# Moving the build of a table of picked positions on VectorE from behind normalised rows to between two steps of the second batch's scores

## The chip, the cores and the metric

The kernel runs on one core of one Trainium2 chip. The metric is the time of one execution on the device in microseconds (us); lower is better. Before the change three runs took 340.24, 340.25 and 340.36 us (median 340.25).

## The reference

Sparse attention with a window and a few global positions is followed by a two-layer network with softplus between the layers. Cut to what matters:

```
B, H, S, D = 8, 8, 576, 64;  8 global positions (global_idx);  window = 32
scores = (q @ k.T) / sqrt(D)
mask = (|i - j| <= window) | is_global[i] | is_global[j]
attn = softmax(where(mask, scores, -1e9))
x = (attn @ v), heads side by side: 4608 tokens x 512
out = softplus(x @ w_in) @ w_out          # 512 -> 2048 -> 512
```

## The kernel before

**Tiles and stages.** The 4608 tokens are cut into 9 phases of 512 tokens. A phase is four steps (n) of four blocks of 32 rows, each with all eight heads. One step of the attention goes through all engines in turn:

- TensorE computes the scores of the step into PSUM (s, L1106).
- VectorE adds the mask and writes the sum to SBUF (st, L1110, two per step), then takes row maxima (m, L1123).
- GpSimd subtracts the maxima (st, L1129).
- ScalarE takes exponentials (st, L1146).
- VectorE sums and inverts (sm, L1153; rs, L1155).
- GpSimd multiplies by the inverse: these are the normalised rows (pn, L1161). There are two buffers of them.
- VectorE transposes them (pt, L1170).
- TensorE multiplies the transposed rows with the values (xo, L1280), once for several steps together. VectorE and ScalarE cast the result (xT, L733).

The rows of the global positions have scores of their own (sg, L999; pg, pgt, ov, odd, vg). Behind xo, the network runs on TensorE (h, L1315, then o, L1326), with softplus on ScalarE (g, L1321). The steps of the attention of the next phase lie between the matmuls of the network of this one.

**Loading.** SyncE's queue loads q and k of batches 2 to 7 and v of batches 2 to 7 as 32-bit numbers (stage). GpSimd and ScalarE cast them to 16 bits (qb, kb, vb; L733, L730, L726), VectorE transposes q and k (qx, L851; kx, L855). GpSimd's queue brings the weights, the first two batches' v (vb, L477) and most of the output (L1338).

**The table of picked positions.** From batch 2 on, the keys and queries of the eight global positions are picked out of kb and qb by a matmul with a table of zeros and ones (pick, L904). `make_pick` (L597 to L606) builds this table once for all batches, with eight instructions on VectorE: a memset of the table (L545, by the helper `clear`), three small operations (L599 to L601), and four comparisons (L604), one for each quarter of the partitions, of positions (posK) with the global indices (gf), both in SBUF:

```
for r in range(R):
    V.tensor_tensor(out=pick[quad(r)]...[:, :, r * NG:(r + 1) * NG],
                    in0=posK[quad(r)]..., in1=gf[quad(r)]..., op=OP.is_equal)
```

Its first reader is the picking of batch 2 (`pck`, L898).

**What sets the order.** The kernel registers some 1700 pieces of work with their dependences, and a table of numbers, `ORDER`, says in which order they are taken: a number is five times the piece, plus the engine (0 TensorE, 1 ScalarE, 2 VectorE, 3 GpSimd, 4 DMA). `make_pick` is piece 37, registered at L1421, so that its number is 187: piece 37 on VectorE. `_Order.run` (L202) walks through the table, gives each piece a planned time from costs (1800 ns for `make_pick`) and a PSUM bank, and emits the pieces in the order of planned times. Every engine executes its instructions strictly in that order; semaphores hold an instruction until its inputs are there.

Of the kernel before, what the change touches and what calls it, by code (L numbers as in the profile page):

```python
# [307 lines left out]
def kernel(  # L308
# [61 lines left out]
        690, 1111, 1116, 986, 1031, 1040, 648, 653, 658, 663, 668, 783, 193, 542, 562, 1021, 1071, 1026, 1076, 1045, 700, 710, 720, 730,  # L370
        1036, 677, 697, 687, 717, 567, 1056, 1051, 706, 771, 1080, 1085, 740, 737, 1720, 727, 1091, 1732, 1096, 750, 760, 776, 1160, 1727,
        766, 746, 1140, 1165, 855, 757, 1145, 871, 1151, 1171, 1156, 866, 1176, 862, 877, 1765, 1810, 1180, 1360, 1320, 1822, 1737, 1772, 1777,
        1817, 1782, 1240, 1365, 1370, 1375, 1325, 1185, 1200, 1205, 1245, 1210, 1215, 1330, 1335, 1196, 1236, 1191, 1250, 1900, 1912, 1855, 1867, 1351,
        1226, 1255, 1346, 1356, 1341, 1120, 1125, 1280, 1285, 1450, 1290, 1295, 1231, 1266, 1271, 1276, 1131, 1261, 1301, 1221, 1311, 1136, 1316, 1907,
        1862, 788, 1965, 1455, 1460, 1465, 1380, 1630, 1385, 1635, 1470, 793, 798, 1948, 1953, 1306, 1640, 1540, 1390, 1645, 1475, 1480, 1650, 1655,
        1545, 1395, 1400, 1660, 1550, 1485, 1743, 1958, 1963, 1788, 1490, 1495, 1405, 1410, 1415, 1500, 1917, 1827, 1833, 1972, 1872, 1878, 1746, 1976,
        1982, 1665, 1985, 1505, 1420, 1791, 1425, 1510, 1670, 1675, 1430, 1435, 1680, 1515, 1752, 1797, 1758, 1803, 1991, 1881, 1997, 2001, 1762, 2005,
        2017, 1836, 1923, 2021, 2744, 2026, 2011, 1520, 1525, 1555, 1560, 1565, 1570, 1887, 1842, 1532, 1807, 1442, 2140, 2060, 1685, 2145, 2065, 2070,
        2150, 2180, 1848, 1893, 2185, 1575, 1580, 2155, 2075, 2190, 1585, 2100, 2105, 2110, 2195, 1926, 2086, 2081, 2161, 2096, 187, 1590, 1595, 2176,
        2115, 2136, 2126, 2171, 2166, 2131, 1600, 1605, 1610, 1690, 1695, 1700, 1448, 2758, 1705, 2380, 2385, 1615, 2201, 2206, 2091, 2121, 1852, 1897,  # L380
        2030, 2035, 1932, 2749, 2390, 2395, 2400, 1712, 2047, 2057, 2753, 2041, 2051, 2405, 2410, 2415, 2270, 2310, 2420, 2763, 1938, 1718, 2766, 2994,
        2216, 2211, 2777, 2772, 2780, 2786, 2276, 2260, 2790, 2266, 2796, 2370, 2230, 2802, 1942, 2316, 2376, 1621, 2236, 2805, 2850, 2220, 2250, 2340,
# [1123 lines left out]
```

## Time and profile before

| | |
|---|---|
| median of three runs | 340.25 us (340.24 to 340.36) |
| profiled execution | 341.66 us, of which the span is 339.9 us |
| TensorE matmul busy | 323.5 us, 95% of the span |
| VectorE busy | 230.6 us, 68% |
| ScalarE busy | 218.5 us, 64% |
| GpSimd busy | 204.7 us, 60% |
| granted TensorE clock, mean | 0.990 |

The span runs from the first to the last instruction of the profiled execution; the rest of its time lies around it. PE is TensorE's matmuls, PEld its weight loads, DVE is VectorE, ACT ScalarE, POOL GpSimd, SP SyncE, and a q behind the name is the engine's queue. A row of a timeline has the start in us from the span's start, the duration in us, engine, line, operation, output<-inputs, shape, the number of instructions merged in it, and in brackets the idle time of the engine ahead of it with what ended it. A row of waits has the engine and line that waited, what released it, the total in us, how often, and the longest. A wait that no semaphore in the profile explains is put down to "issue". The shares in the chain say what the path that ended last consisted of. Spans on GpSimd are rough, and busy time on TensorE is not work at its peak, since matmuls are pipelined.

### The profile page before, as it was taken

How to read it: one execution, taken by the hardware profiler on the slowest of the kernel's cores; microseconds unless marked ns; L12 is line 12 of the kernel's file. 1: busy time of each engine (PE TensorE's matmuls, PEld its weight loads, DVE VectorE, ACT ScalarE, POOL GpSimd, SP SyncE). 2: the span in 40 equal slices, each digit the busy share in tenths (PEclk: the TensorE clock that was granted, in tenths of full speed). 3: DMA queues.
4: the chain of work that ended last, by engine and by line, in shares of the span. 5: the costliest groups of instructions: out<-in, count | busy, mean ns of one | idle time of the engine just before them, and what ended most of it. 6: DMA issues, size and time to landing. Idle time of an engine off the chain costs nothing.

```text
span 339.9 us, 12052 instructions
## 1 busy us (share of the span) xinstructions
PE 323.5 (95%) x5277; PEld 173.5 (51%) x5277; DVE 230.6 (68%) x400; ACT 218.5 (64%) x438; POOL 204.7 (60%) x185
## 2 busy tenths in 40 slices
PE   8889979967999999899999999999999999999996
PEld 3547866543545545454445445444544454454543
DVE  6886768898796899974888558597689563342000
ACT  4789628542596969377866674898258656934531
POOL 6899746795189449679578679587058609060000
PEclk9999999995999999999999999999999999999999
DMA  6999999999903979989989991341001002000102
GB/s 181 167 187 170 169 165 142 153 185 184 183 10 62 170 153 209 151 166 194 206 158 175 204 202 52 73 128 38 4 33 62 3 35 93 33 31 33 64 33 91
DMA packets 172391, 40.36 MB, mean 119 GB/s; under 512 B 161460, under 2 KB 168884, under 8 KB 172340
## 3 DMA queue, kind: packets, MB, share of 16 engines
q1 hardware_dynamic: 145908, 23.61, 40.7%
q0 software_dynamic: 24560, 12.85, 25.4%
q10 hardware_dynamic: 1872, 3.15, 2.4%
q8 instruction: 41, 0.67, 0.9%
q14 instruction: 10, 0.08, 0.1%
HBM read 36.71 MB, written 9.44 MB: 136 GB/s over the span
## 4 chain that ended last, share of the span: by engine, by line
PE 86%; DVE 7%; DMA 2%; SPq 2%; ACT 2%; issue 1%
PE o L1326 36%; PE h L1315 36%; PE xo L1280 5%; PE s L1106 3%; DVE pick L604 2%; DMA stage<-in_q_dram 2%; PE ov L1028 2%; ACT st L1142 1%; PE pick L904 1%; DVE pt L1170 1%; SPq L530 1%; PE sg L999 1%; SPq L523 1%; DVE m L1121 1%; DVE sm L1153 1%
## 5 line engine op out<-in xcount | busy, mean ns | idle before, releaser
L1326 PE MATMUL o<-wout,g 128*128 128x512 bf16 (+1 forms) x592 | 138.5, 376 | 1.2 <-issue 1.2
L1321 ACT ACTIVATE g<-h 128x512 bf16<-128x512 f32 (+3 forms) x192 | 83.9, 496 | 47.1 <-PE h L1315 44.2
L1161 POOL TENSOR_TENSOR pn<-st,rs 128x1024 bf16<-128x1024 f32 (+1 forms) x36 | 64.8, 1810 | 42.4 <-DVE rs L1155 40.0
L1326 PEld LDWEIGHTS <-g 128*128 128x128 bf16 x592 | 56.0, 98 | 63.5 <-issue 3.4
L1129 POOL TENSOR_TENSOR st<-st,m 128x1024 f32<-128x1024 f32 x32 | 60.6, 1898 | 40.7 <-DVE m L1123 36.7
L1315 PE MATMUL h<-xT,winx 128*128 128x512 bf16 (+3 forms) x384 | 73.5, 326 | 1.5 <-issue 1.5
L1315 PE MATMUL h<-xT,win 128*128 128x512 bf16 (+3 forms) x384 | 72.4, 328 | 0.0
L1153 DVE TENSOR_REDUCE sm<-st 128x8 f32<-128x1024 f32 x32 | 38.3, 1195 | 16.8 <-ACT st L1146 16.8
L1315 PEld LDWEIGHTS <-win 128*128 128x128 bf16 x384 | 33.6, 98 | 31.2 <-issue 2.6
L1315 PEld LDWEIGHTS <-winx 128*128 128x128 bf16 x384 | 33.8, 98 | 30.0 <-issue 0.4
L1110 DVE TENSOR_TENSOR st<-s,mask 128x512 f32<-128x512 f32 x64 | 40.9, 676 | 9.7 <-PE s L1106 9.5
L1123 DVE TENSOR_REDUCE m<-st 128x8 f32<-128x1024 f32 x32 | 38.3, 1204 | 0.2
L1146 ACT ACTIVATE st<-st 128x1024 f32<-128x1024 f32 x32 | 32.9, 1051 | 1.4 <-POOL st L1129 1.2
L1170 DVE STREAM_TRANSPOSE pt<-pn 128x512 int32<-128x512 int32 x36 | 24.8, 697 | 12.3 <-POOL pn L1161 12.1
L733 ACT CAST xT<-xo 128x512 bf16<-128x512 f32 (+3 forms) x23 | 10.3, 493 | 24.7 <-PE xo L1280 24.5
L733 ACT COPY osb<-o 128x512 f32<-128x512 f32 (+1 forms) x22 | 12.6, 572 | 18.6 <-PE o L1326 17.6
L733 DVE CAST xT<-xo 128x512 bf16<-128x512 f32 (+3 forms) x25 | 12.5, 540 | 16.4 <-PE xo L1280 16.4
L1338 POOL DMA_DIRECT2D out_dram<-osb x24 | 13.8, 575 | 10.3 <-ACT osb L733 5.5
L1106 PE MATMUL s<-kx,qx 64*32 64x128 bf16 x1152 | 16.1, 219 | 0.4 <-ACT kx L733 0.3
L1106 PEld LDWEIGHTS <-qx 64*32 64x32 bf16 x1152 | 11.9, 91 | 7.9 <-issue 4.8
L1321 ACT ACT_TABLE_LOAD x12 | 15.4, 1283 | 0.8 <-PE h L1315 0.6
L742 PE MATMUL warm<-vb 128*128 128x512 bf16 x49 | 14.1, 433 | 1.3 <-DVE vb L562 1.3
(136 smaller groups left out, 337.2 us busy)
## 6 DMA issues: line engine op xcount, KB each, us to landing
stage<-in_k_dram SPq DMA_DIRECT2D x48, 144.0 KB, 4.1
stage<-in_q_dram SPq DMA_DIRECT2D x48, 144.0 KB, 4.2
stage<-in_v_dram SPq DMA_DIRECT2D x48, 144.0 KB, 4.0
out_dram<-osb POOLq DMA_DIRECT2D x24, 256.0 KB, 3.3
out_dram<-osb ACTq DMA_DIRECT2D x11, 256.0 KB, 2.0
wout<-in_moe_w_out_dram POOLq DMA_DIRECT2D x4, 512.0 KB, 8.8
vb<-in_v_dram POOLq DMA_DIRECT2D x16, 72.0 KB, 6.4
stage<-in_k_dram SPq DMA_DIRECT2D x2, 512.0 KB, 5.5
```

What stands on the lines that cost most here:

```text
L733: {"ACT": nc.scalar.copy, "DVE": V.tensor_copy, "POOL": nc.gpsimd.tensor_copy}[e](out, in_)
L1106: nc.tensor.matmul(out=PS["s", n, h][quad(c), x, :], lhsT=qx[b % 2][rows(g), a, j * BL:(j + 1) * BL], rhs=kx[b % 2][rows(g), a, e0 * BL:(e ...
L1110: V.tensor_tensor(out=PS["st", n][:, h, :, :], in0=PS["s", n, h][:, :, :], in1=mask[:, h, j0:j0 + PB, :, :].rearrange("p j s i -> p j (s i ...
L1123: V.reduce_max(out=m[:], in_=flat(PS["st", n], h0, h1), axis=AX)
L1129: on(e).tensor_tensor(out=t, in0=t, in1=over(PS["m", n, y][:], SL * BL), op=OP.subtract)
L1146: nc.scalar.activation(out=t, in_=t, func=AF.Exp)
L1153: V.reduce_sum(out=sm[:], in_=flat(PS["st", n], h0, h1), axis=AX)
L1161: on(e).tensor_tensor(out=PS["pn", n][:, :, :, h0:h1].rearrange("p x s h -> p h x s"), in0=PS["st", n][:, h0:h1], in1=PS["rs", n, y][:].re ...
L1170: V.transpose(out=bass.AP(base.tensor, base.offset, ap=[list(base.ap[0]), [2 * STEP, PB // 2], [STEP + BL // 2, 2], [1, SL * BL]]), in_=PS ...
L1315: nc.tensor.matmul(out=h[:, :], lhsT=w_in_t[c // 4][:, kd, c % 4 * P:(c % 4 + 1) * P], rhs=PS["xT", m][:, kd, lo:hi], start=(kd == 0), sto ...
L1321: nc.scalar.activation(out=PS["g", m, c][:, lo:hi], in_=PS[key][:, lo_of(c, hi - lo)], func=AF.Softplus)
L1326: nc.tensor.matmul(out=PS["o", m, ns, a][:, :], lhsT=PS["g", m, kf][:, ns * P:(ns + 1) * P], rhs=w_out_t[kf // 4][:, kf % 4, a:z], start=( ...
```

## The change

One number of the table `ORDER` is moved to an earlier place; every other number keeps its order. Cut to its core:

```
-        1817, 1782, 1240, 1365, ...
+        1817, 187, 1782, 1240, 1365, ...
...
-        ... 2086, 2081, 2161, 2096, 187, 1590, 1595, 2176,
+        ... 2086, 2081, 2161, 2096, 1590, 1595, 2176,
```

The eight instructions of `make_pick` are the only ones that change place on any engine. The instructions of TensorE, ScalarE, GpSimd and SyncE stand in the same order as before. The two halves of the second batch's global scores (sg) trade their PSUM banks with each other, because the planned times differ; all other banks are the same.

The old place, on VectorE, is at the end of the network of phase 0. In before: osb is the copy of a finished output tile, pt the transposes of normalised rows of the steps whose values TensorE takes next, sm the sum of the step behind.

```order
L733 COPY osb<-o 128x512
L545 MEMSET pick 128x288
L599 TENSOR_SCALAR place<-pos,pi 128x32
L600 TENSOR_SCALAR pi<-pi 128x1
L601 TENSOR_SCALAR posK<-pos,pi 128x18
L604 TENSOR_TENSOR pick<-posK,gf 32x18x8 x4
L1170 STREAM_TRANSPOSE pt<-pn 128x2x2x128 x2
L1153 TENSOR_REDUCE sm<-st 128x8
```

The same place on VectorE in the changed kernel:

```order
L733 COPY osb<-o 128x512
L1170 STREAM_TRANSPOSE pt<-pn 128x2x2x128 x2
L1153 TENSOR_REDUCE sm<-st 128x8
L1155 RECIPROCAL rs<-sm 128x8
L733 COPY osb<-o 128x512
```

The two transposes now follow the copy of the output tile directly.

The new place, on VectorE, lies some twenty rows earlier, among the scores of the second batch. In before: st is a masked add, m a maximum of its rows.

```order
L1123 TENSOR_REDUCE m<-st 128x8
L1110 TENSOR_TENSOR st<-s,mask 128x512 x3
L1123 TENSOR_REDUCE m<-st 128x8
L1110 TENSOR_TENSOR st<-s,mask 128x512 x4
L1123 TENSOR_REDUCE m<-st 128x8 x2
```

The same place on VectorE in the changed kernel:

```order
L1110 TENSOR_TENSOR st<-s,mask 128x512 x3
L545 MEMSET pick 128x288
L599 TENSOR_SCALAR place<-pos,pi 128x32
L600 TENSOR_SCALAR pi<-pi 128x1
L601 TENSOR_SCALAR posK<-pos,pi 128x18
L604 TENSOR_TENSOR pick<-posK,gf 32x18x8 x4
L1123 TENSOR_REDUCE m<-st 128x8
L1110 TENSOR_TENSOR st<-s,mask 128x512 x4
```

The eight instructions stand between three masked adds and the maximum that reads two of them; the next four masked adds come behind that maximum, as before.

14 rows, old and new, of the table ORDER are left out of this document.

## The prediction

> **What bounds the kernel now.** I read the page's chain first, then the list of waits, then the timelines around the one long wait.
>
> The page's span, and the chain that ended last by engine:
>
> ```profile
> span 339.9 us, 12052 instructions
> PE 86%; DVE 7%; DMA 2%; SPq 2%; ACT 2%; issue 1%
> ```
>
> TensorE sets the end: 86% of the chain is its own work. VectorE's 7% is where it can be held up. The waits of TensorE's matmuls (engine, line, released by; total us, times, longest):
>
> ```profile
> PE xo L1280 <- DVE pt L1170: 5.5, 1, 5.5
> PE h L1315 <- issue: 1.5, 1, 1.5
> PE ov L1028 <- DVE pgt L1018: 1.3, 1, 1.3
> ...
> PE o L1326 <- issue: 1.2, 1, 1.2
> ```
>
> One wait of 5.5 us is as long as the next four together, and it happens once: value products (xo) waiting for VectorE's transposes of normalised rows (pt). The chain in order of time shows what stood ahead of those transposes (start us, us, what):
>
> ```profile
> 70.58 1.62 DVE pick L604
> 72.21 4.76 DVE pick L604
> 77.64 1.32 DVE pt L1170 x2
> 79.00 1.62 PE xo L1280 x95
> 80.61 2.67 PE o L1326 x6
> 83.28 1.83 PE h L1315 x8
> ...
> 85.33 0.69 PE pick L904 x35
> ...
> 88.48 0.68 PE s L1106 x64
> ...
> 97.21 0.65 PE h L1315 x4
> 97.86 0.65 PE o L1326 x3
> ...
> 108.85 1.56 PE xo L1280 x145
> ```
>
> The table of picked positions (pick, L604) is on the chain, directly ahead of the transposes, and xo starts 0.04 us after they end. On TensorE itself the pause is clean:
>
> ```profile
> 71.17 2.32 PE L1326 MATMUL o<-wout,g 128*128 128x512 bf16 x10
> 79.00 0.54 PE L1280 MATMUL xo<-pt,vg 32*64 32x384 bf16 x8 [5.50 <-DVE pt L1170]
> ```
>
> Work ends at 73.49, nothing until 79.00. So the table sits on the path, and what the change is worth is read from this pause and from what follows it.
>
> **What the table costs, and why so much.** VectorE's timeline for its first and last parts, and the four comparisons of L604 by duration (ns min/median/max):
>
> ```profile
> 69.88 0.30 DVE L545 MEMSET pick<- 128x288 int32 x1
> ...
> 70.58 7.03 DVE L604 TENSOR_TENSOR pick<-posK,gf 32x144 bf16<-32x144 f32 x4
> ```
>
> ```profile
> L604 DVE TENSOR_TENSOR pick<-posK,gf x4: 301/962/4765, 70.6 to 77.3; 32x144 bf16<-32x144 f32 x4
> ```
>
> Equal comparisons take from 0.30 to 4.77 us. GpSimd's timeline over the same stretch says why:
>
> ```profile
> 68.28 3.76 POOL L1161 TENSOR_TENSOR pn<-st,rs 128x1024 bf16<-128x1024 f32 x2 [1.30 <-DVE rs L1155]
> 71.98 0.64 POOL L1338 DMA_DIRECT2D out_dram<-osb  x1
> 72.61 2.85 POOL L733 CAST kb<-stage 128x1152 bf16<-128x1152 f32 x2
> 75.43 1.44 POOL L730 TENSOR_SCALAR qb<-stage 128x1152 bf16<-128x1152 f32 x1
> ```
>
> The first comparison ends at 72.20, just after GpSimd's pn (72.04); the second ends at 76.97, just after GpSimd's casts (76.87). Two of the four were held up by GpSimd. Unhindered, the table is 0.70 us (69.88 to 70.58: memset, L599 to L601) plus four times 0.31 (the shortest and 0.01 between), 1.94 us, against the 7.73 us (69.88 to 77.61) that it took.
>
> **The old place, emptied.** The transposes then wait only for pn. The second pn ends at 72.04 and one transpose takes half of 1.32 us, so both are done at about 72.8, 0.7 us before TensorE finishes at 73.49. The whole 5.50 us go, and what is late next is nothing at this point.
>
> The pause costs more than its length. Granted clock of TensorE in two stretches behind it (length and each engine's busy time, then the clock):
>
> ```profile
> 79.00:83.00 4.00, 4.00 (x126) 2.31 (x126) 2.74 (x6) 2.36 (x5) 2.54 (x3) 0.50 1.06 169
> 83.00:87.00 4.00, 4.00 (x82) 2.16 (x81) 2.71 (x4) 1.12 (x5) 1.55 (x2) 0.85 1.01 231
> ```
>
> Half clock for 4.0 us, and 0.85 over the next 4.0 means 1.2 us more: 5.2 us at half speed. By the chain's rows, six o took 2.67 us where three take 0.65 at full clock (six: 1.30), a loss of 1.37. Eight h took 1.83 where four take 0.65 (eight: 1.30), a loss of 0.53. The xo took 1.62 against 1.56 at 108.85, a loss of 0.06: so small a matmul is hardly bound by the clock. Together 1.96 us. [...]
>
> Is the work behind the pause ready that early? Two covers are thin:
>
> ```profile
> 80.75 1.01 DVE L733 CAST xT<-xo 128x384 bf16<-128x384 f32 x2
> ```
>
> ```profile
> 81.39 1.52 ACT L726 ACTIVATE qb<-stage 128x1152 bf16<-128x1152 f32 x1
> ```
>
> VectorE's casts of xT end at 81.76, 1.15 us after xo ends (80.61); h needs them, and the six o between hide them for 1.30 us at full clock: 0.15 us to spare. ScalarE's cast of qb ends at 82.91, 2.30 us after xo; TensorE's picking (L904) comes 1.30 + 1.30 + 0.22 = 2.82 us after it: 0.5 us to spare. GpSimd's casts end at 76.87 in any case; the picking would come at 73.50 + 1.6 + 2.8 = 77.9. I leave 0.15 us for these.
>
> **The new place.** VectorE and GpSimd there, in before:
>
> ```profile
> 46.98 1.87 DVE L1110 TENSOR_TENSOR st<-s,mask 128x512 f32<-128x512 f32 x3
> 48.78 1.21 DVE L1123 TENSOR_REDUCE m<-st 128x8 f32<-128x1024 f32 x1
> 51.77 2.48 DVE L1110 TENSOR_TENSOR st<-s,mask 128x512 f32<-128x512 f32 x4 [1.79 <-PE s L1106]
> ...
> 59.05 0.48 DVE L1016 STREAM_TRANSPOSE pgt<-pg 128x288 int32<-128x288 int32 x1 [0.50 <-ACT pg L1011]
> ```
>
> ```profile
> 49.00 2.64 POOL L477 DMA_DIRECT2D vb<-in_v_dram  x4
> ...
> 56.59 1.90 POOL L1129 TENSOR_TENSOR st<-st,m 128x1024 f32<-128x1024 f32 x1 [3.03 <-DVE m L1123]
> ```
>
> The table now goes between the masked adds (end 48.85) and the maximum, into a stretch where VectorE then idles 1.79 us, waiting for TensorE's scores. At 1.94 us it overshoots by 0.15. Queued behind it are the maximum, the next masked adds, and everything after. Who waits for those: GpSimd's subtraction of that maximum, which cannot start before its four DMA issues end at 51.64, so it starts some 0.3 us later and then has 3.03 us of idle time behind it; and TensorE, whose next matmuls take PSUM banks that the masked adds read. The tightest of these banks is that of this o, which the second masked add frees at about 51.77 + 2 × 0.62 (a quarter of the four's 2.48) = 53.0:
>
> ```profile
> 53.65 0.38 PE L1326 MATMUL o<-wout,g 128*128 128x512 bf16 x1
> ```
>
> So a delay of up to 0.6 us costs TensorE nothing, and VectorE's 0.50 us of idle time at 59.05 takes it back. I cost the new place at nothing, bounded by 1.9 us (first rival). The change adds no instruction and moves no DMA; GpSimd's, ScalarE's and SyncE's queues keep their order.
>
> **The sum.** 5.50 + 1.96 − 0.15 = 7.3 us. The profiled execution took 341.66 us (339.9 of span and 1.8 around it), which is 1.4 us above the median of the runs, 340.25; neither the pause nor the clock belongs to that difference, so I take 7.3 off the median: **333.0 us**, with 332.2 to 333.6 as the forecast's own range.
>
> **The rivals.** First, the comparisons are blocked at the new place too, now by GpSimd's DMA issues (49.00 to 51.64). For: the second comparison started at 72.21, while GpSimd was issuing a DMA (71.98 to 72.61), and could have ended before the cast; it did not. Against, a comparison-like VectorE operation with both inputs in SBUF, at full speed inside eight DMA issues:
>
> ```profile
> 8.22 0.31 DVE L635 TENSOR_TENSOR near<-near,dup 128x144 f32<-128x144 f32 x1
> ```
>
> ```profile
> 7.81 5.60 POOL L477 DMA_DIRECT2D vb<-in_v_dram  x8
> ```
>
> If it holds, the comparisons end at 51.64 + 1.24 = 52.9, the maximum at 54.1, and the masked adds start 2.3 us late. TensorE's cover is 0.6 us, so it loses about 1.8: 334.8. Chance 0.12. [...]
>
> Second, the closed-up stretch meets a wait that the pause had hidden, such as TensorE's own supply of instructions: the "issue" waits of 1.5 and 1.2 us above. For: the 208 matmuls that the two clock rows count now follow without a pause ahead of them. Against: only a few such waits in the whole span. Price 1.2 to 1.5 us: about 334.3. Chance 0.15.
>
> Third, nothing is gained because the input loads set the pace later on, so TensorE waits there for what it gained here: about 340. SyncE's queue of loads speaks against it; before the next load it waits for a cast, not the reverse:
>
> ```profile
> SPq L472 <- ACT kb L733: 13.9, 1, 13.9
> ```
>
> It has 13.9 us to give, nearly twice the gain. Chance 0.03.
>
> Fourth, slower: xo was held by something else as well (another operand, a bank), so the pause stays, and the table at its new place holds the masked adds that free the banks. It decides from 0.6 us of delay; with the first rival's blocking it costs up to 1.9 us: 340.3 to 342.2. Against it: xo starts 0.04 us after the transposes. Chance 0.04.
>
> **How the numbers follow.** Forecast 0.66, first rival 0.12, second 0.15, third 0.03, fourth 0.04. The range takes the forecast and the first two: 332.0 (the full 7.46 and a little of the other waits) to 335.2. A measurement can tell about 0.2% (0.7 us) from no change. The forecast and the first two rivals are faster (0.93), with a third of the third's chance 0.94; the rest of the third is same, 0.02; the fourth slower, 0.04.
>
> **What would show it.** Right: L604's four comparisons at 0.30 us each near 49.5 to 50.8; no wait of xo for pt at 73.5; clock 1.00 from 73 to 85; the scores now at 88.48 near 81; all later rows 7.3 us earlier. Wrong: a comparison of over 1 us at the new place (first rival), new "issue" waits between 73 and 90 (second), growing waits for stage loads after 106 (third), xo still idle before 79 (fourth).

## The result and the profile after

| | before | after |
|---|---|---|
| median, runs of the first comparison | 340.31 us (340.24 to 340.49, 4 runs) | 334.19 us (333.60 to 334.54, 4 runs) |
| ratio, 95% interval | | 0.9818 (0.9801 to 0.9835) |
| profiled execution, span | 341.66 us, 339.9 us | 334.54 us, 332.8 us |
| mean granted TensorE clock | 0.990 | 0.999 |

The kernel is 6.1 us faster (5.6 to 6.8 by the interval). The forecast was 333.0 us in a range of 332.0 to 335.2. Timed again at the end with five rounds, the same changed kernel gave 333.47 us against 340.69 us, 7.2 us faster (6.4 to 8.0).

The changed kernel's page, the span and the chain that ended last by engine:

```profile
span 332.8 us, 12010 instructions
PE 87%; issue 3%; DVE 3%; ACT 3%; DMA 2%; SPq 2%; ACTq 0%
```

VectorE's share of the chain fell from 7% to 3%. The 3% of "issue" is mostly not time lost: the trace of after holds 5235 matmuls where that of before holds 5277, as many as its weight loads, so 42 matmul records are missing, and each hole in a run of o reads as a wait of 0.16 us. The waits of after's matmuls, the longest groups:

```profile
PE o L1326 <- issue: 3.8, 17, 1.2
PE h L1315 <- issue: 1.5, 2, 1.3
PE xo L1280 <- issue: 1.3, 1, 1.3
```

The wait of xo for pt, 5.5 us before, isn't in the list at all. TensorE's timeline of after at the old place:

```profile
71.70 2.32 PE L1326 MATMUL o<-wout,g 128*128 128x512 bf16 x10
73.96 0.38 PE L1280 MATMUL xo<-pt,vg 32*64 32x384 bf16 x8
74.15 1.11 PE L1280 MATMUL xo<-pt,vb 32*64 32x32 bf16 x112
75.42 1.24 PE L1326 MATMUL o<-wout,g 128*128 128x512 bf16 x5 [0.16 <-issue]
76.50 0.81 PE L1315 MATMUL h<-xT,win 128*128 128x384 bf16 x4
...
78.10 0.47 PE L904 MATMUL pick<-kb,pick 128*32 128x128 bf16 x18
...
81.25 0.75 PE L1106 MATMUL s<-kx,qx 64*32 64x128 bf16 x64
```

xo follows the ten o without a gap, and the picking follows at 78.10 (forecast 77.9, with work ahead of 70 us standing 0.5 us later in this execution). The granted clock in after (length, busy times of the five engines, clock, DMA):

```profile
74.00:78.00 4.00, 3.84 (x135) 2.48 (x135) 2.55 (x6) 2.54 (x5) 4.00 (x4) 1.00 1.02 211
```

The next 4 us are at 1.00 too: the half clock behind the pause is gone with the pause. VectorE in after, at the new place and then at the old one:

```profile
47.69 1.88 DVE L1110 TENSOR_TENSOR st<-s,mask 128x512 f32<-128x512 f32 x3
49.57 0.30 DVE L545 MEMSET pick<- 128x288 int32 x1
...
50.26 1.24 DVE L604 TENSOR_TENSOR pick<-posK,gf 32x144 bf16<-32x144 f32 x4
51.51 1.22 DVE L1123 TENSOR_REDUCE m<-st 128x8 f32<-128x1024 f32 x1
52.65 2.47 DVE L1110 TENSOR_TENSOR st<-s,mask 128x512 f32<-128x512 f32 x4
...
72.60 0.71 DVE L1170 STREAM_TRANSPOSE pt<-pn 128x512 int32<-128x512 int32 x1 [1.14 <-POOL pn L1161]
```

The same four comparisons by duration (min/median/max ns), and GpSimd meanwhile:

```profile
L604 DVE TENSOR_TENSOR pick<-posK,gf x4: 297/299/304, 50.3 to 51.2; 32x144 bf16<-32x144 f32 x4
```

```profile
49.70 2.65 POOL L477 DMA_DIRECT2D vb<-in_v_dram  x4
```

The table takes 1.94 us (49.57 to 51.51) in place of 7.73, VectorE's 1.79 us of idle time there is used up, and the transposes end at 73.31, 0.65 us ahead of xo. All four comparisons ran inside the DMA issues and none was held.

**Where the time came from.** I cut TensorE's timeline at three marks: the start of the 64 scores near 51 us, the start of xo behind the pause, and the start of batch 2's first scores. The marks of before, besides its xo at 79.00, and then the first mark of after:

```profile
51.09 1.07 PE L1106 MATMUL s<-kx,qx 64*32 64x128 bf16 x64
...
88.41 0.75 PE L1106 MATMUL s<-kx,qx 64*32 64x128 bf16 x64
```

```profile
51.62 1.07 PE L1106 MATMUL s<-kx,qx 64*32 64x128 bf16 x64
```

| execution | scores near 51 to xo | xo to batch 2's scores | both |
|---|---|---|---|
| before | 27.91 | 9.41 | 37.32 |
| after | 22.34 | 7.29 | 29.63 |

The first part lost 5.57 us, the second 2.12, together 7.69. From there to the start of the last run of 56 o it is 238.29 us and 238.34: nothing is given back later. The 0.6 us by which the profiled spans fall short of 7.7 lie ahead of these marks: the scores near 51 us start at 51.62 in after and at 51.09 in before, behind "issue" waits that differ between the two executions (the 1.3 us of xo above stands at 32.0 us; before waits 0.16 us there).

### The profile page after: what moved, and what is told of

It reads as the page before. It is cut to its first block, busy times and chain, and to the rows that moved or that the text cites. A ratio compares the mean times of both kernels' runs of the same rounds, so it can differ in the third digit from the quotient of the medians.

```text
span 332.8 us, 12010 instructions
## 1 busy us (share of the span) xinstructions
PE 316.5 (95%) x5235; PEld 172.6 (52%) x5277; DVE 225.0 (68%) x400; ACT 218.7 (66%) x438; POOL 204.9 (62%) x185
## 4 chain that ended last, share of the span: by engine, by line
PE 87%; issue 3%; DVE 3%; ACT 3%; DMA 2%; SPq 2%; ACTq 0%
PE o L1326 37%; PE h L1315 37%; PE xo L1280 4%; PE s L1106 4%; DMA stage<-in_q_dram 2%; PE ov L1028 2%; ACT st L1142 1%; PE pick L904 1%; SPq L530 1%; PE sg L999 1%; SPq L523 1%; DVE m L1121 1%; ACT g L1321 1%; PE tr L882 1%; PE pick L917 1%
## 5 line engine op out<-in xcount | busy, mean ns | idle before, releaser
L1326 PE MATMUL o<-wout,g 128*128 128x512 bf16 (+1 forms) x564 | 131.9, 373 | 4.7 <-issue 3.8
L1315 PE MATMUL h<-xT,win 128*128 128x512 bf16 (+3 forms) x378 | 71.4, 325 | 0.5 <-issue 0.2
L1280 PE MATMUL xo<-pt,vb 32*64 32x96 bf16 (+2 forms) x1328 | 14.0, 210 | 1.3 <-issue 1.3
```

The costliest lines, as they stand in the source:

```text
L1280: nc.tensor.matmul(out=PS["xo", v_, hd // 2][half * D:(half + 1) * D, (x - X0) * BL:(z - X0) * BL], lhsT=lhs, rhs=rhs, start=start and not ...
L1315: nc.tensor.matmul(out=h[:, :], lhsT=w_in_t[c // 4][:, kd, c % 4 * P:(c % 4 + 1) * P], rhs=PS["xT", m][:, kd, lo:hi], start=(kd == 0), sto ...
L1326: nc.tensor.matmul(out=PS["o", m, ns, a][:, :], lhsT=PS["g", m, kf][:, ns * P:(ns + 1) * P], rhs=w_out_t[kf // 4][:, kf % 4, a:z], start=( ...
```

## The experiments

Theory: the pause existed because the table, at its old place, was held by GpSimd's work; moved, it costs 1.9 us in time that VectorE had free. Against it stood that the new place has a price of its own, that the pause was held by something else as well, and that the half clock is worth less than I took it for. All times are set against runs of the kernel before on the same chip.

### Both kernels again (e1_before_again, e2_after_again)

No edit; one execution each.

> The kernel before, unchanged, for a second profile of it. The saving measured 6.1 us between medians and 7.1 us between the two profiled executions, where 7.3 was forecast. If the first profile of before caught an unusually long pause, xo's wait for pt is 4 to 5 us here and the span about 338.5. If the pause is always the same and the difference lies in the waits for instructions, the wait for pt is 5.4 to 5.6 us again and the "issue" waits of TensorE differ by 1 us or so from the first profile.

> The changed kernel, unchanged, for a second profile. No wait of xo for pt at about 73.5 and four comparisons of 0.30 us each in either theory. If the waits for instructions make up the spread of 1 us between runs, the "issue" waits near 32 and 48 us differ from the first profile by about the difference of the two spans.

Measured: 342.33 us (span 340.6) for before, 334.0 us (332.3) for after. The pause is 5.5 us again and the old comparisons take 301/961/4765 ns; in after they take 297/299/304. In before, the "issue" waits moved:

```profile
PE xo L1280 <- issue: 2.0, 2, 1.3
PE h L1315 <- issue: 1.8, 1, 1.8
PE o L1326 <- issue: 1.3, 1, 1.3
```

These sum to 5.1 us where the first execution of before had 1.5 + 1.2 + 0.6 = 3.3. The span grew by only 0.7 of these 1.8 us: the first xo starts 0.8 us earlier in e1 (24.29 against 25.05), and the half clock costs 0.25 less (below). In e2 the waits near 32 and 48 us sum to 2.30 us where the first execution of after had 2.61, 0.3 us less, and the span is 0.5 shorter. The pause is the kernel's, with the same length each time; the microsecond or two by which executions differ comes from elsewhere, and in before also from the half clock behind it.

### A second, unread table at the old place (e3_both_places)

The changed kernel, plus a copy of make_pick into tiles of its own that nothing reads:

```
+    o.add({"DVE": (1800, 1890)}, lambda e: make_pick_2(), ...)
-    ... 2161, 2096, 1590, ...
+    ... 2161, 2096, 8582, 1590, ...
```

> The changed kernel, with a second table (of its own tiles, read by nobody) built at the old place with the same eight instructions. Theory (the table at the old place is the pause, because GpSimd holds up its comparisons there): the comparisons take 1 to 5 us again, xo waits about 5.5 us for pt, and the time is that of before, 340.3 us, or up to 0.4 above it. Rival (the pause had another cause, which the change removed by the way, such as the exchanged PSUM banks): about 334.2 us and no such wait.

Measured: 341.13 us (10 runs), ratio to before 1.0020 (0.9990 to 1.0051). Its waits of TensorE, and its comparisons at the old place (here L620) and the new (L604):

```profile
PE xo L1296 <- DVE pt L1186: 5.5, 1, 5.5
```

```profile
L620 DVE TENSOR_TENSOR pick<-posK,gf x4: 300/960/4792, 69.9 to 76.6; 32x144 bf16<-32x144 f32 x4
```

```profile
L604 DVE TENSOR_TENSOR pick<-posK,gf x4: 296/298/304, 48.3 to 49.2; 32x144 bf16<-32x144 f32 x4
```

The same instructions in one execution are 0.30 us each in one place and up to 4.79 in the other, and the old place alone brings the whole loss back. Nothing that reads the table is needed for that.

### The pause filled with matmuls (e4_warm_pause)

The kernel before; ahead of the waiting xo, TensorE runs 24 matmuls whose result is overwritten:

```
+                if v_ == 4:
+                    for x in range(24):
+                        nc.tensor.matmul(out=PS["xo", v_, x % KD][:, :], lhsT=w_in_t[0][:, 0, 0:P], rhs=w_in_t[0][:, 1, :], start=True, stop=True)
```

> The kernel before, with 24 matmuls of 128x512 on TensorE ahead of the xo that waits; their results are overwritten. 24 times 0.216 us is 5.2 us, so they fill the pause and do not lengthen it. Theory (the half clock behind the pause costs about 2.0 us on top of its 5.5): the clock stays at 1.00 and the time falls by 2.0 us to 338.3 us. [...] Rival (the clock costs nothing there, something else is late behind the pause anyway): 340.3.

Measured: 338.77 us (10 runs), ratio 0.9931 (0.9902 to 0.9960), 1.4 to 3.3 us faster than before. TensorE's timeline, and the clock behind:

```profile
72.84 5.34 PE L1269 MATMUL xo<-win 128*128 128x512 bf16 x24
78.55 0.38 PE L1283 MATMUL xo<-pt,vg 32*64 32x384 bf16 x8 [0.37 <-DVE pt L1170]
...
79.77 1.47 PE L1329 MATMUL o<-wout,g 128*128 128x512 bf16 x6
```

```profile
78.00:82.00 4.00, 3.63 (x133) 2.46 (x133) 3.29 (x6) 2.13 (x3) 1.99 (x2) 1.00 1.10 176
```

xo still waits for the transposes until 78.55, but the six o behind take 1.47 us as a run where before's take 2.74, and from xo to batch 2's scores it is 7.29 us, as in after. The median is 2.0 us below that of before: this is the half clock's share alone.

### The table earlier still (e5_earlier)

The kernel before, with the table moved from its old place into an idle stretch of VectorE near 30 us; the number at its new place:

```
-    ... 836, 1010, 537, 842, ...
+    ... 836, 1010, 537, 187, 842, ...
```

> The table built still earlier, in a stretch of 2.5 us near 30 us in which VectorE waits for TensorE and GpSimd only issues DMAs. Theory (the change's place costs TensorE nothing): the same as the changed kernel within its spread, 333.6 to 334.5 us. Rival (the change's place costs part of the 1.2 us that the saving stayed behind the forecast, since the table overshoots VectorE's idle time there): 333.0 us.

Measured: 333.89 us (4 runs), ratio 0.9804 (0.9784 to 0.9824). The comparisons (295/298/304 ns) run at 30.3 us. From the scores near 51 us to xo it is 22.33 us, in after 22.34: TensorE needs as long with the table at the new place as without it there. The new place is free.

### A second table at the new place (e6_twice_new)

The unread table of e3, now directly behind the first:

```
+    1817, 187, 8582, 1782, ...
```

> The changed kernel with a second table (of its own tiles, read by nobody) directly behind the first at the new place: 1.94 us more of VectorE ahead of the maximum. Theory (TensorE has 0.6 us of cover there, of which the one table uses 0.15): TensorE loses 1.94 - 0.45 = 1.5 us, 335.7 us. Rival (VectorE's idle time behind takes it all): 334.2 us. Rival (no cover at all): 336.1 us.

Measured: 335.51 us (4 runs), ratio 0.9842 (0.9799 to 0.9884). TensorE's timeline:

```profile
53.76 0.61 PE L1331 MATMUL h<-xT,winx 128*128 128x128 bf16 x8 [1.71 <-DVE st L1126]
```

TensorE waits 1.71 us for the bank that a masked add frees. Counted from the start of the scores near 51 us, the four masked adds behind the table start at 0.68 us in e5 (51.18 less 50.50), at 1.03 in after (52.65 less 51.62) and at 3.26 here (53.03 less 49.77): one table delays them by 0.35 us, two by 2.58. From those scores to xo it is 22.33, 22.34 and 24.35 us. So of 2.58 us of delay TensorE loses 2.02, and the cover is 0.56 us, where the working had 0.6. The o that the prediction called tightest starts at 54.36, just after the second of the four masked adds ends (54.30).

### The table directly behind the transposes (e7_behind_pt)

```
-    ... 2161, 2096, 187, 1590, ... 2121, 1852, 1897,
+    ... 2161, 2096, 1590, ... 2121, 1852, 1897, 187,
```

> The kernel before, with the table directly behind the two transposes in place of ahead of them. xo no longer waits for it. Theory (GpSimd holds the comparisons until 76.9 us wherever they stand in this stretch, and VectorE's next work waits in turn): the sum, the output copy and the casts of xT come about 3.5 us late, h waits for xT, and half of the gain is lost: about 337 us. Rival (only the transposes were on the path): 334.2 us.

Measured: 340.77 us (10 runs), ratio 1.0003 (0.9976 to 1.0031): I had expected a gain, and there is none. TensorE, then VectorE, then GpSimd:

```profile
72.67 0.38 PE L1280 MATMUL xo<-pt,vg 32*64 32x384 bf16 x8
...
75.21 0.33 PE L1315 MATMUL h<-xT,win 128*128 128x384 bf16 x1
80.31 1.12 PE L1315 MATMUL h<-xT,win 128*128 128x384 bf16 x3 [4.77 <-DVE xT L733]
```

```profile
72.26 3.94 DVE L599 TENSOR_SCALAR place<-pos,pi 128x32 bf16<-128x32 f32 x1
...
79.71 1.01 DVE L733 CAST xT<-xo 128x384 bf16<-128x384 f32 x2
```

```profile
71.86 2.88 POOL L733 CAST kb<-stage 128x1152 bf16<-128x1152 f32 x2
74.70 1.46 POOL L730 TENSOR_SCALAR qb<-stage 128x1152 bf16<-128x1152 f32 x1
```

xo goes at once, and the pause comes behind the next o and the first h, because the casts of xT are queued on VectorE behind the table. And what is held now isn't a comparison: it is L599, with one tensor and a scalar per partition as inputs, for 3.94 us, until GpSimd's last cast ends at 76.16. The four comparisons behind it take 1.24 us together. The expectation had only a delay of about 3.5 us; TensorE's pause is 4.77 us, and it halves the clock again, from 77.89 to 84.72: from the scores near 51 us to batch 2's it is 36.57 us, where before has 37.32 and after 29.63.

### Comparisons with one tensor input (e8_one_input)

The kernel before; each comparison becomes eight with a scalar per partition as the second operand:

```
-            V.tensor_tensor(out=pick[quad(r)]...[:, :, r * NG:(r + 1) * NG], in0=posK..., in1=gf..., op=OP.is_equal)
+            for y in range(NG):
+                V.tensor_scalar(out=pick[quad(r)]...[:, :, r * NG + y],
+                                in0=posK[quad(r)]..., scalar1=gf[quad(r), y:y + 1], scalar2=None, op0=OP.is_equal)
```

> The kernel before, the table at its old place, but each of the four comparisons replaced by eight with one tensor input and a scalar per partition (32 of 32x18 in place of 4 of 32x144). Theory (GpSimd holds only operations with two inputs in SBUF): they are not held, the table ends near 74 us, xo waits 1 to 2 us in place of 5.5, the clock stays up, and the time is about 334.5 to 335.5 us. Rival (any work of the table is held there, or the place itself is too late): about 340 us.

Measured: 344.57 us (4 runs), ratio 1.0112 (1.0060 to 1.0164): slower, where I had expected nearly the changed kernel's time. The 32 comparisons by duration:

```profile
L605 DVE TENSOR_SCALAR pick<-posK,gf x32: 248/251/4803, 70.3 to 80.8; 32x18 bf16<-32x18 f32 x32
```

One is held from 71.87 to 76.67 (GpSimd's casts run from 72.36 to 76.61), the first for 1.52 us, and the other thirty take 0.25 us each. These overlap, with a start every 0.14 us or so: of the 10.76 us from the first start to the last end (70.32 to 81.08) 6.3 are the two holds and 4.4 the rest, against 1.24 for the four. TensorE's pause grows to 9.23 us. So it gains nothing because of the hold, and is slower than before because of its 32 instructions. That comparisons are held only because they read two tensors is refuted.

### No casts on GpSimd (e9_no_pool_casts)

The kernel before with the table at its old place; batch 2's two casts of kb go to ScalarE, and the cast of qb behind GpSimd's next pn:

```
-    ... 1700, 1448, 2758, 1705, ... 2121, 1852, ... 2057, 2753, 2041, ... 2763, 1938, ...
+    ... 1700, 1448, 1705, ... 2121, 2756, 2751, 1852, ... 2057, 2041, ... 1938, 2763, ...
```

> The kernel before, the table at its old place, but GpSimd's three casts of batch 2 taken away from that stretch: the two of kb go to ScalarE ahead of the casts of xT, that of qb stays on GpSimd but behind the next normalised rows. The earlier runs showed that an operation of the table is held there whatever its number of inputs. Theory (it is GpSimd's run of casts that holds it): the first comparison is held until GpSimd's normalised rows end, the other three take 0.30 us, the transposes end near 74.4 on the first profile's clock, xo waits about 1 us in place of 5.5, the clock stays up, and the time is 335 to 336.5 us (the qb cast is 0.5 us late for the picking). Rival (the place is too late for the transposes in any case): about 340 us.

Measured: 334.96 us (4 runs), ratio 0.9850 (0.9818 to 0.9882). The comparisons, and TensorE:

```profile
L604 DVE TENSOR_TENSOR pick<-posK,gf x4: 298/302/1619, 69.6 to 71.9; 32x144 bf16<-32x144 f32 x4
```

```profile
73.59 0.38 PE L1280 MATMUL xo<-pt,vg 32*64 32x384 bf16 x8 [1.03 <-DVE pt L1170]
```

Without the casts beside it the 4.8 us of the second comparison are gone; the first is still held by pn (1.62 us), and the pause is 1.03 us, behind which the clock stays up (mean of the run 0.998). GpSimd's run of casts is what held the table, shown by taking it away with the table unmoved.

### Ahead of the three masked adds (e10_ahead_of_adds)

Against the changed kernel, the table goes ahead of the three masked adds that it stood behind, beside a GpSimd subtraction:

```
-    ... 1822, 1737, 1772, ... 1817, 187, 1782, ...
+    ... 1822, 1737, 187, 1772, ... 1817, 1782, ...
```

> The table three masked adds earlier than in the changed kernel, directly behind the maximum of the second batch's first step, so that its operations meet GpSimd's subtraction (1.9 us) in place of GpSimd's DMA issues. Theory (an operation of the table is held while GpSimd computes from SBUF, not while it issues DMAs): one operation is held until the subtraction ends, 1.2 us or so; the masked adds come some 3.2 us late in place of 1.9, TensorE's scores and the matmuls behind them wait 0.8 to 1.5 us, and the time is 335 to 335.5 us. Rival (no hold): all four comparisons at 0.30 us, and 334.0 us.

Measured: 333.88 us (4 runs), ratio 0.9798 (0.9768 to 0.9829). VectorE, then GpSimd:

```profile
46.92 1.79 DVE L599 TENSOR_SCALAR place<-pos,pi 128x32 bf16<-128x32 f32 x1
...
49.02 1.24 DVE L604 TENSOR_TENSOR pick<-posK,gf 32x144 bf16<-32x144 f32 x4
```

```profile
46.78 1.89 POOL L1129 TENSOR_TENSOR st<-st,m 128x1024 f32<-128x1024 f32 x1 [7.20 <-DVE m L1123]
48.63 2.64 POOL L477 DMA_DIRECT2D vb<-in_v_dram  x4
```

The first operation is held until the subtraction ends at 48.67, as expected; then, beside the DMA issues, L601 takes 0.23 us and the four comparisons 1.24, as in e5. The next four masked adds start 2.44 us behind the scores near 51 us (53.20 less 50.76), 1.76 later than in e5, and from those scores to xo it is 23.54 us, 1.21 more: again 0.55 us were covered. The same o starts at 54.53, after the second of these masked adds ends (54.48). So the loss that I expected for TensorE came, but the time missed: the median can't be told from the changed kernel's. The profiled execution does show the loss, with 334.98 us against 333.83 in e11 on the same chip; the other three, 333.22 to 334.19, end 0.3 above the slowest of e11.

### The changed kernel, five rounds (e11_after_timed)

> The changed kernel, unchanged, timed again beside more runs of before on one chip, since the runs of before spread from 339.2 to 344.7 us and those of the changed kernel only from 333.6 to 334.5. By stages of the profiles (TensorE's part from the second batch's last scores to the next batch's first) the saving is 5.6 us of pause and 1.3 to 2.1 of half clock, 6.9 to 7.7 us: the median should come out 6.5 to 7.3 us below that of before. If the first measurement's 6.1 us is the true saving, 6.1 or less.

Measured: 333.47 us (332.42 to 333.86, 6 runs) against 340.69 (338.83 to 341.61, 11 runs), ratio 0.9789 (0.9765 to 0.9812), 7.2 us saved. From the scores near 51 us to batch 2's it is 29.62 us, in the first profile of after 29.63. No version tried beats it: e5 and e10, at 333.9, are the same within their spread.

## Why the prediction was right, point by point

- **The pause of 5.50 us goes in full.** It did: 5.57 us by the marks; xo without a wait.
- **The half clock is worth 1.96 us.** The profile pair has 2.12; e4 alone shows 1.4 to 3.3 by time. One part was misread. TensorE in before, behind xo's start at 79.00:

```profile
80.55 2.74 PE L1326 MATMUL o<-wout,g 128*128 128x512 bf16 x6
83.08 1.38 PE L1315 MATMUL h<-xT,win 128*128 128x384 bf16 x4
```

From start to start, xo took 1.55 us, the six o 2.53 and the eight h 1.87 (the next o starts at 84.95); in e4, with a full clock, they took 1.22, 1.31 and 1.30. So xo was bound by the clock after all and lost 0.33 us, not 0.06, and the six o lost 1.22, not 1.37: the xo at 108.85 that I compared with is a larger piece of work, 160 matmuls in the timeline where the one at 79.00 has 120.

The size isn't fixed either. From xo to batch 2's scores it is 9.41, 9.16 and 8.59 us in before, e1 and e3, against 7.29 with a full clock: losses of 2.12, 1.87 and 1.30 behind the same pause. That 1.96 came so near was in part luck: I read it from one execution. The reason is in fine windows of the clock, of before, then of e3, where the last figures are clock, DMA share and GB/s:

```profile
77.20:77.40 0.20, 0.00 (x0) 0.00 (x0) 0.19 (x2) 0.00 (x0) 0.00 (x0) 1.00 1.36 213
77.40:77.60 0.20, 0.00 (x0) 0.00 (x0) 0.20 (x1) 0.00 (x0) 0.00 (x0) 0.50 1.29 200
...
84.20:84.40 0.20, 0.20 (x3) 0.10 (x1) 0.20 (x2) 0.00 (x0) 0.20 (x1) 0.94 0.71 200
```

```profile
75.00:75.20 0.20, 0.00 (x0) 0.00 (x0) 0.20 (x1) 0.00 (x0) 0.20 (x1) 0.60 0.00 0
...
81.80:82.00 0.20, 0.20 (x2) 0.07 (x1) 0.00 (x0) 0.20 (x1) 0.20 (x1) 0.83 1.09 197
```

Before is at half clock from 77.40 to 84.22, e3 from 75.04 to 81.87: 6.82 and 6.83 us. e1 and e7 give 6.83 and 6.82, and e8, with its pause of 9.2 us, 10.24. What differs is how far into the pause the half clock begins: 3.90 us in before, 3.39 in e1, 2.26 in e3, 2.35 in e7 and 5.16 in e8. So it lasts beyond the end of the pause for 5.22 us in before, 4.72 in e1, 3.56 in e3, 4.41 in e7 and 6.17 in e8. What sets its start is not shown. The 5.2 us at half speed that the prediction read from before are one case of a range, 3.56 to 6.17 us.
- **The new place costs nothing.** Shown by e5. The masked adds come 0.35 us later in the first execution of after and 0.13 and 0.17 in e2 and e11, where 0.15 was forecast, within a cover of 0.56 (e6, e10). The first rival (held by DMA issues) falls: four comparisons at 0.30 us inside them. The row at 72.21 that spoke for it is answered by e9: there the second comparison starts at 71.27, inside the issue of the same output DMA (71.04 to 71.68), but with no casts behind that, and takes 0.30 us. So in before the casts held it, though the profile has them start 0.40 us after it (72.61); how they do so ahead of their start stays open, and spans on GpSimd are rough.
- **Thin covers, 0.15 us.** None of it was needed: xo to batch 2's scores is 7.29 us in after, where the only wait in between, of 0.16 us, is a missing record, and the same in e4, where GpSimd's casts had 5 us more. VectorE's casts of xT end at 76.35 in after and h starts at 76.50: the 0.15 us to spare that the prediction counted.
- **"Two of the four were held up by GpSimd."** Right, by e9. In e8's theory I took it as a matter of operations with two inputs in SBUF, an assumption of mine; that was too narrow: TENSOR_SCALARs were held for 3.94 us in e7, 4.80 in e8 and 1.79 in e10. It didn't enter the sum.
- **333.0 us.** The 1.2 us between it and the first measurement aren't a wait in the closed-up stretch (second rival): there was none of over 0.16 us between 73 and 85 us. The runs of either kernel differ: over all comparisons the changed kernel's lay between 332.42 and 334.54, those of before between 338.83 and 344.70. The forecast of 7.3 us lies above the interval of the first comparison (5.6 to 6.8) and inside that of e11 (6.4 to 8.0); the marks say 7.7. Part of the spread is the length of TensorE's "issue" waits near 32, 43, 49 and 135 us, and for before how far into the pause the half clock begins; what sets those waits stays open.
- **Third and fourth rivals.** xo was held by nothing else. The queue of loads, in SyncE's waits of after, still waits for a cast, for 5.0 us where it was 13.9, so it had the gain to give:

```profile
SPq L472 <- ACT kb L733: 5.0, 1, 5.0
```

## What to carry to other kernels

Before you put a small VectorE job into an idle stretch, look at what GpSimd runs beside it: the same eight instructions took 1.9 us beside DMA issues and 7.7 beside arithmetic. Then look at what is queued behind the job, since moving it by two instructions (e7) only moved the pause to the next reader. Price a pause of TensorE like this one with the half clock behind it: the pauses of 4.77 to 9.23 us here all brought it, that of 1.03 us in e9 did not, and its cost was a range (1.3 to 2.1 us for the same pause of 5.5), not a number.

## What the runs showed that I had not expected

- **A held VectorE operation wasn't let in between two casts of GpSimd.** In e8 it waits 4.80 us, through three casts of about 1.4 us back to back; in e7 3.94 us. So the length of the run of casts counted, not of one. It isn't shown for every run of GpSimd: at the old place L599 took 0.12 us (70.10 to 70.22) while one pn gave way to the next.
- **One tensor input is enough to be held.** Held were TENSOR_TENSOR 32x144 (4.77 us), TENSOR_SCALAR 128x32 (3.94) and 32x18 (4.80), all from SBUF to SBUF and all from f32 to bf16; but in e10 L600, from f32 to f32, started 0.03 us behind L599 and took 1.76 us beside its 1.79. The two TENSOR_SCALAR also read a scalar per partition from SBUF; one without it was not tested by itself. Other VectorE work ran beside the same GpSimd work at its own length: in after, a transpose inside pn (68.82 to 72.57) took 0.70 us and row sums inside the casts (73.15 to 77.47) 1.18, the means of all 36 and 32 of that shape being 0.70 and 1.20; two casts out of PSUM inside the casts took 1.02 together, beside a pn in before 1.01:

```profile
69.12 0.70 DVE L1170 STREAM_TRANSPOSE pt<-pn 128x512 int32<-128x512 int32 x1
...
73.24 1.18 DVE L1153 TENSOR_REDUCE sm<-st 128x8 f32<-128x1024 f32 x1
...
75.33 1.02 DVE L733 CAST xT<-xo 128x384 bf16<-128x384 f32 x2
```

Why L599 to L601 (0.12, 0.14 and 0.23 us, beside pn, at the old place) were not held stays open.
- **An eighth of the elements did not take an eighth of the time.** The comparisons of 32x18 in e8 took 0.25 us each and started some 0.14 us apart; those of 32x144, with eight times the elements, took 0.30 and started 0.31 apart.
